# Talking-heads attention with two dense blocks: mixing weights spread by matmuls, first heads turned in column halves, two loads moved among stores

## The chip, the core and the metric

The kernel runs on one core of a Trainium2 chip. The metric is the device time of one execution in microseconds. Durations of single instructions and transfers come from one profiled execution.

## The reference

The attention works on 2 batches, 12 heads, 448 positions and 64 elements for each head, and mixes the heads twice: the scores before the softmax, and the softmax after it.

```python
scores = scale * np.matmul(q, k.transpose(0, 1, 3, 2))
scores = np.einsum('bhij,hg->bgij', scores, w_pre)
attn = softmax(scores)                                  # over j
attn = np.einsum('bhij,hg->bgij', attn, w_post)
x = np.matmul(attn, v)                                  # then (batch, position) x (head, element): 896 x 768
...
xn = x / sqrt(mean(x * x) + 1e-06) * rms_g
y = (silu(xn @ w_gate) * (xn @ w_val)) @ w_out          # 768 -> 1536 -> 768
out = elu(y @ w_in) @ w_out2                            # 768 -> 2048 -> 768
```

All inputs and the output are float32. `w_pre` and `w_post` are 12 x 12.

## The kernel before

The order of the work on every engine is written out by hand: an engine executes its instructions in program order, and a wait at one holds all that is behind it on that engine. All large transfers are issued by SyncE, in order, into one queue; the small ones of the start are issued by ScalarE.

**Opening.** `load_small` loads `w_pre` and `w_post` (12 x 12 each, into `wpp`) and two copies of them broadcast to 128 partitions (`wide`, `wpb`). `load_first` loads the six pairs of heads of q and k of the first batch, 224 KB each, alternately k and q. A position is split as 112 partitions times 4 chunks. The tiles of k lie as (chunk, head, element), so that each piece of a transfer is 64 floats, 256 bytes. The tiles of q lie as (head, chunk, element), so that a piece is 1024 bytes, and `q_beside` copies each of them on VectorE into the order of k. `busy(n)` puts n transposes of the identity, whose result nobody uses, on TensorE: 20 before the first pair, 8, 6, 4 and 4 between the turnings of the first two pairs.

Then a loop of eight trips runs over the pairs. Trip i turns k and q of pair i (`turned`, line 444: four transposes each, 112 positions by 128 columns that are two heads), and for pair i - 2 makes the premixed scores of the first two groups directly (`direct`, line 484, with q multiplied by the weights `wpq`, `mixed_q`) and the raw scores of the first 112 rows (`scores`, line 497). `follow` issues what ScalarE and VectorE have to do with the results. The matrices `m1` and `m2`, block diagonal copies of the weights for groups of 10 rows, come out of `select`, `repeat`, `copies` and `blocks`, in trip 1. `select` takes the largest value in each column of `w_post` from `wpb`.

**Way of the scores.** Raw scores of two heads and 112 rows are copied to a tile (`scores_out`; seven tiles in turn, four named `st_w` and three `st`) and stored in DRAM, `s_d`, 392 KB each; six of them make a block of 112 rows. `load_group` loads two groups (2 x 10 rows, all heads, 420 KB) back as `sg`, with four such tiles. Groups 0 and 1 don't take this way. Groups 2 to 5 are loaded after the opening (`AT_ONCE = 2` loads).

**Steps.** After the opening come the softmax of groups 0 and 1 (`soft`), six pairs of scores of the second row block (the loop over `EARLY`, one store each), and then the steps, counted by t from -4. Step t contains, among others, in this order, the load of groups t + 7 and t + 8 where t + 7 is even (AHEAD = 7), the premixing matmuls of group t + 1 (lines 582 or 585 to 587), the split of group t + 3 on ScalarE (`g_split`, line 574, even groups only), the exponential of group t (line 602) and the postmixing of group t - 3 (line 661). So groups 6 and 7 are loaded in step -1, as the first of the steps' loads, and split in step 3; groups 14 and 15 are loaded in step 7 and split in step 11. A window of 70 rows is closed by the product with v (`av`, line 697, f32, the two heads of a pair into the two halves of the output partitions). In between, pairs of heads of the second batch are loaded (`load_qk`, line 392, 256-byte pieces), turned and scored, and v is loaded (line 380). The two dense blocks follow.

Of the kernel before, what the change touches and what calls it, by code (L numbers as in the profile page):

```python
# [9 lines left out]
F32 = mybir.dt.float32  # L10
# [12 lines left out]
def block_kernel(  # L23
# [15 lines left out]
    nc = tc.nc  # L39
# [58 lines left out]
    def slot(p, *dims):  # L98
        a, n = taken[0], 1
        for d in dims:  # L100
            n *= d
        taken[0] += n
        t = setup[:p, a:a + n]
        return t.rearrange("p (a b) -> p a b", a=dims[0]) if len(dims) > 1 else t
# [1 line left out]
    m1 = slot(GP, GI, H)  # L106
    m2 = slot(GP, GI, H)
    wpp = slot(H, 2, H)
    wpb = slot(P, H * H)
    wpq = slot(P, H // 2, H)  # L110
    g_sb = const.tile([P, KD], F32, name="g_sb")
    g_dn = const.tile([P, KD], F32, name="g_dn")
# [2 lines left out]
    m2l = const.tile([GP, H, GI], F16, name="m2l")  # L115
    vsc = const.tile([P, KD], F32, name="vsc")

    def load_small(wide):
        nc.scalar.dma_start(out=wpp[:, 0], in_=w_pre)
        nc.scalar.dma_start(out=wpp[:, 1], in_=w_post)  # L120
        nc.scalar.dma_start(
            out=wide, in_=w_pre.rearrange("h g -> (h g)").unsqueeze(0).to_broadcast([P, H * H])
        )
        nc.scalar.dma_start(
            out=wpb, in_=w_post.rearrange("h g -> (h g)").unsqueeze(0).to_broadcast([P, H * H])
        )

    def mixing(m1f, m1h, m1l):

        selr, cmax, rcm, m2p = slot(H, GI, H), slot(P, H), slot(P, H), slot(GP, H, GI)  # L130
        a1 = m1.rearrange("p i g -> p (i g)")
# [238 lines left out]
    def attention(actx):  # L370
# [26 lines left out]
        def load_first():  # L397

            n_pair = 2 * NCH * D
            room = [ap.tile([CP, NCH * H * WMAX], F32, tag="at", name="qk0", bufs=2) for _ in range(2)]  # L400
            for p in range(NP):
                for j, (src, tag) in enumerate(((k, "kt"), (q, "qt"))):
                    a = (p % 3 * 2 + j) * n_pair
                    t = room[p // 3][:, a:a + n_pair]
                    if tag == "kt":
                        t = t.rearrange("p (c h d) -> p c h d", h=2, c=NCH)
                        nc.sync.dma_start(out=t, in_=pair_of(src, 0, p))
                    else:
                        t = t.rearrange("p (h c d) -> p h c d", h=2, c=NCH)
                        nc.sync.dma_start(  # L410
                            out=t, in_=src[0, 2 * p:2 * p + 2].rearrange("h (p c) d -> p h c d", c=NCH)
                        )
                    qk_sb[0, p, tag] = t

        def q_beside(p):

            t = ap.tile([CP, NCH, 2, D], F32, tag="qt", name="qt", bufs=2)
            nc.vector.tensor_copy(out=t, in_=qk_sb[0, p, "qt"].rearrange("p h c d -> p c h d"))
            qk_sb[0, p, "qt"] = t

        idle_ps = []

# [16 lines left out]
        def turned(b, p, tag):  # L439

            t = qk_sb.pop((b, p, tag))
            ps = ps_a()
            for c in range(NCH):
                nc.tensor.transpose(
                    out=ps[:, c * CP:(c + 1) * CP], in_=t[:, c].rearrange("p h d -> p (h d)"),
                    identity=ident[:CP, :CP],
                )
            hi, lo = parts_of(b, p, tag)
            on_act.append(lambda: nc.scalar.activation(out=hi, in_=ps[:, :S], func=ACTF.Copy))
            if b == 0 and tag == "qt":  # L450
                on_dve.append(lambda: mixed_q(p, ps))
            on_dve.append(
                lambda: nc.vector.tensor_tensor(out=lo, in0=ps[:, :S], in1=hi.bitcast(F32), op=ALU.subtract)
            )
# [328 lines left out]
        m1f = ap.tile([GP, GP], F32, tag="m1f", name="m1f", bufs=1)  # L783
        m1h = ap.tile([GP, GP], F32R, tag="m1h", name="m1h", bufs=1)
        m1l = ap.tile([GP, GP], F32R, tag="m1l", name="m1l", bufs=1)
        select, repeat, copies, blocks, _, pre, post = mixing(m1f, m1h, m1l)
        wide = ap.tile([P, KD, WMAX], F32, tag="sq", name="wide", bufs=1)[:, :3].rearrange("p k i -> p (k i)")[:, :H * H]
        load_small(wide)
        load_first()
        busy(20)  # L790
        q_beside(0)
        for s in range(2):
            nc.vector.tensor_copy(
                out=wpq[s * D:(s + 1) * D],
                in_=wide.rearrange("p (k s g) -> p s k g", s=2, g=H)[s * D:(s + 1) * D, s],
            )
        for i in range(NP + 2):
            if i < NP:
                turned(*pairs[i], "kt")
                if i < 2:  # L800
                    busy(8 - 4 * i)
                turned(*pairs[i], "qt")
                if i < 2:
                    busy(6 - 2 * i)
            if i == 1:
                select()
                repeat()
            if i > 1:
                direct(0, i - 2)
                scores(0, i - 2, 0, True)  # L810
            if i + 1 < NP:
                q_beside(i + 1)
            follow()
            if i == 1:
                copies()
                blocks()
        idle_ps.clear()
# [15 lines left out]
        for j in range(EARLY):  # L833
            if j in (0, 3):
                g_postmix(0, j // 3)
                g_out(0, j // 3)
            hq.pop(0)()
            follow()
        fast = len(hq)
        hq += [f for i in range(NP, 2 * NP) for f in turn(i)]  # L840
        turns = len(hq)
# [346 lines left out]
```

## Time and profile before

| | |
|---|---|
| median of 3 runs | 765.9 us (764.99 to 766.69) |
| profiled execution | 766.09 us |
| its span, first to last instruction | 764.3 us |
| TensorE busy | 746.3 us, 98% |
| VectorE busy | 549.2 us, 72% |
| ScalarE busy | 438.9 us, 57% |
| GpSimd busy | 100.3 us, 13% |
| mean granted TensorE clock | 0.994 of 2.4 GHz |
| moved by DMA | 103.68 MB, mean 136 GB/s |

The span is 1.8 us shorter than the profiled execution. A matmul's busy time overlaps with that of the next one, so a high share of TensorE is not the share of its peak. The chain of waits is followed back from the last instruction; idle time of an engine that is not on it costs nothing. In the rows below PE is TensorE's matmul, PEld its weight load, DVE VectorE, ACT ScalarE, POOL GpSimd, and SP SyncE; a q behind the name is the sequencer. L and a number is a line of the kernel.

### The profile page before, as it was taken

The page shows a single profiled execution, that of the slowest core. Times are in us where ns is not written, and L with a number is a line of the kernel's source. Part 1 is how long each engine was busy: PE and PEld are TensorE (multiplying, and loading weights), DVE is VectorE, ACT ScalarE, POOL GpSimd, SP SyncE. Part 2 cuts the span into 40 slices and gives each one's busy share as a digit, 9 for nine tenths or more (in the row PEclk, how much of TensorE's full clock was granted, in tenths as well). Part 3 has the DMA queues.
Part 4 walks back from the last instruction along what each step waited for, and adds up shares of the span by engine and source line. Part 5 has one row for each costly group of instructions (what it writes and reads, how often), then busy time and mean ns, then how long its engine had stood idle before and what let it go on. Part 6 is the DMA issues. An engine that isn't in the chain of part 4 may idle for free.

```text
span 764.3 us, 14562 instructions
## 1 busy us (share of the span) xinstructions
PE 746.3 (98%) x5740; PEld 590.6 (77%) x5740; DVE 549.2 (72%) x1094; ACT 438.9 (57%) x916; POOL 100.3 (13%) x122
## 2 busy tenths in 40 slices
PE   7979999999999999999999999999999999999997
PEld 6647887777777755555555599999999999999997
DVE  4757998988998757787886766554888778723731
ACT  4548788988988716666667423232766665312310
POOL 2122454443445300000000000000000000000000
PEclk9989999999999999999999999999999999999999
DMA  7699976878772013433332233241334334533602
GB/s 172 184 325 305 187 186 194 242 201 239 223 191 57 2 42 126 123 94 114 124 124 82 86 122 124 83 122 51 120 121 125 109 98 125 164 85 82 168 30 73
DMA packets 86616, 103.68 MB, mean 136 GB/s; under 512 B 20549, under 2 KB 77077, under 8 KB 86549
## 3 DMA queue, kind: packets, MB, share of 16 engines
q1 hardware_dynamic: 86213, 102.61, 47.0%
q8 instruction: 45, 0.74, 0.4%
q10 hardware_dynamic: 336, 0.15, 0.1%
q14 instruction: 22, 0.18, 0.1%
HBM read 80.72 MB, written 22.02 MB: 134 GB/s over the span
## 4 chain that ended last, share of the span: by engine, by line
PE 89%; DVE 4%; ACT 3%; DMA 3%; issue 1%; SPq 1%; ACTq 0%
PE psa_t L202 13%; PE psa_t L204 13%; PE psa_t L203 13%; PE pst_t L661 6%; PE psv_t L697 5%; PE psa_t L582 4%; PE psa_t L1144 4%; PE psa_t L1142 4%; PE psa_t L1143 4%; PE psa_t L497 4%; PE psf_t L202 3%; PE psf_t L204 3%; PE psf_t L203 3%; PE psa_t L585 2%; PE psf_t L1143 1%; PE psf_t L1142 1%
## 5 line engine op out<-in xcount | busy, mean ns | idle before, releaser
L661 PEld LDWEIGHTS <-eh 120*112 120x112 f16 x720 | 66.7, 131 | 25.4 <-issue 16.2
L257 ACT ACTIVATE whl<-w 128x768 fp32r<-128x768 f32 x44 | 37.2, 846 | 85.5 <-DVE w L251 74.9
L229 ACT ACTIVATE w<-raw 128x768 f32<-128x768 f32 x68 | 61.6, 908 | 25.4 <-DVE whl L309 18.9
L261 DVE TENSOR_TENSOR whl<-w,whl 128x768 fp32r<-128x768 f32 x44 | 42.2, 959 | 45.3 <-ACT whl L257 45.3
L204 PE MATMUL psa_t<-x2h,whl 128*128 128x448 f32 x192 | 70.5, 367 | 0.0
L202 PE MATMUL psa_t<-x2h,whl 128*128 128x448 f32 x192 | 70.1, 365 | 0.0
L203 PE MATMUL psa_t<-x2l,whl 128*128 128x448 f32 x192 | 69.8, 364 | 0.0
L575 POOL TENSOR_TENSOR sl<-sg,sh 120x448 fp32r<-120x448 f32 (+1 forms) x44 | 54.6, 1241 | 109.4 <-ACT sh L574 104.0
L602 ACT ACTIVATE e<-psa_t,nmax 120x448 f32<-120x448 f32 (+1 forms) x89 | 57.1, 642 | 19.3 <-DVE rs L617 16.0
L640 DVE SCALAR_TENSOR_TENSOR el<-e,rs,eh 120x448 f16<-120x448 f32 (+1 forms) x90 | 66.1, 734 | 0.1
L251 DVE SCALAR_TENSOR_TENSOR w<-w,raw 128x768 int32<-128x768 int32 x68 | 65.2, 959 | 1.1
L245 DVE SCALAR_TENSOR_TENSOR raw<-raw 128x768 int32<-128x768 int32 x68 | 65.7, 966 | 0.0
L661 PE MATMUL pst_t<-m2h,el 120*112 120x120 f16 x360 | 63.0, 218 | 1.6 <-DVE el L640 1.5
L661 PE MATMUL pst_t<-m2h,eh 120*112 120x120 f16 x360 | 63.2, 218 | 0.7 <-DVE eh L633 0.5
L661 PE MATMUL pst_t<-m2l,eh 120*112 120x120 f16 x360 | 63.1, 217 | 0.0
L301 ACT ACTIVATE w<-w,gs 128x128 f32<-128x128 f32 x144 | 44.6, 392 | 23.2 <-DVE gs L290 23.2
L594 DVE TENSOR_REDUCE nmax<-psa_t 120x1 f32<-120x448 f32 (+1 forms) x89 | 54.5, 612 | 0.2 <-PE psa_t L587 0.2
L673 ACT ACTIVATE at<-pst_t 112x480 f32<-112x480 f32 (+1 forms) x90 | 52.5, 583 | 3.5 <-PE pst_t L661 3.2
L697 PE MATMUL psv_t<-at,vs 112*64 112x70 f32 (+3 forms) x1344 | 54.2, 228 | 0.0
L1142 PE MATMUL psa_t<-whl,gh 128*128 128x384 f32 x160 | 54.0, 338 | 0.0
L1143 PE MATMUL psa_t<-whl,gh 128*128 128x384 f32 x160 | 54.0, 338 | 0.0
L1144 PE MATMUL psa_t<-whl,gl 128*128 128x384 f32 x160 | 54.0, 338 | 0.0
(158 smaller groups left out, 1900.4 us busy)
## 6 DMA issues: line engine op xcount, KB each, us to landing
raw<-in_moe_w_out_dram SPq DMA_DIRECT2D x28, 768.0 KB, 4.4
sg<-s_d SPq DMA_DIRECT2D x43, 420.0 KB, 6.1
s_d<-st SPq DMA_DIRECT2D x33, 392.0 KB, 3.6
raw<-in_moe_w_in_dram SPq DMA_DIRECT2D x16, 768.0 KB, 4.6
raw<-in_moe_w_gate_dram SPq DMA_DIRECT2D x12, 768.0 KB, 4.5
raw<-in_moe_w_val_dram SPq DMA_DIRECT2D x12, 768.0 KB, 4.4
s_d<-st_w SPq DMA_DIRECT2D x15, 392.0 KB, 4.9
vs<-in_v_dram SPq DMA_DIRECT2D x12, 224.0 KB, 6.4
```

The lines of the kernel that those rows point to most:

```text
L202: nc.tensor.matmul(out=ps, lhsT=wh(kk), rhs=xh_(kk), start=(first and kk == 0), stop=False)
L203: nc.tensor.matmul(out=ps, lhsT=wh(kk), rhs=xl_(kk), start=False, stop=False)
L204: nc.tensor.matmul(out=ps, lhsT=wl(kk), rhs=xh_(kk), start=False, stop=(last and kk == nk - 1))
L229: nc.scalar.activation(out=w, in_=raw.bitcast(F32)[:, :, 1], func=ACTF.Abs if small else ACTF.Copy, scale=REBASE)
L245: nc.vector.scalar_tensor_tensor(out=lo, in0=hi, scalar=SIGN, in1=lo, op0=ALU.bitwise_and, op1=ALU.bitwise_or)
L251: nc.vector.scalar_tensor_tensor(out=wi, in0=wi, scalar=3, in1=lo, op0=ALU.logical_shift_left, op1=ALU.bitwise_or)
L640: nc.vector.scalar_tensor_tensor(out=el[:r], in0=e32[:r], scalar=rs[:r], in1=eh[:r], op0=ALU.mult, op1=ALU.subtract)
L661: nc.tensor.matmul(out=o, lhsT=lhs[:r, c * CP:(c + 1) * CP], rhs=rhs[:r, :, :ni], start=(n == 0), stop=(n == 2),)
L697: nc.tensor.matmul(out=psx[s * D:(s + 1) * D, kk, :n], lhsT=vs[b, kk][:, s, c, :], rhs=at[:, c, hh, :n], start=(c == 0), stop=(c == NCH - 1),)
L1142: nc.tensor.matmul(out=o, lhsT=gh[:, kk, tk], rhs=wh[:, j], start=first, stop=False)
L1143: nc.tensor.matmul(out=o, lhsT=gh[:, kk, tk], rhs=wl[:, j], start=False, stop=False)
L1144: nc.tensor.matmul(out=o, lhsT=gl[:, kk, tk], rhs=wh[:, j], start=False, stop=end)
```

## The change

- `load_small` keeps the two 12 x 12 loads. The broadcasts are no longer transfers: `spread_small` builds selectors from the identity and two products of them with the weights on VectorE, multiplies on TensorE (K = 12, 72 and 144 columns), copies `wpq` out and leaves `wpb` in PSUM, where `select` reads it. `select` now comes before the loop, `repeat`, `copies` and `blocks` in trip 0. `spread_small` stands behind the 20 fillers and ahead of the first turning on TensorE.
- The tiles of k of the first batch lie as those of q, in 1024-byte pieces; `q_beside` goes.
- `turned` of the first batch makes, for each chunk and each head, a matmul of 112 x 64 stationary data with the identity, f32, into partitions 0 to 63 or 64 to 127, in place of one transpose for both heads. The second batch keeps its loads and transposes.
- In the loop over `EARLY`, the loads of groups 6 and 7 and of groups 8 and 9 are issued after the third and the sixth store of the second row block; `AT_ONCE` becomes 4, and the steps' loads begin with groups 10 and 11.

```diff
--- before.py
+++ after.py
@@ -106,7 +106,6 @@
     m1 = slot(GP, GI, H)
     m2 = slot(GP, GI, H)
     wpp = slot(H, 2, H)
-    wpb = slot(P, H * H)
     wpq = slot(P, H // 2, H)
     g_sb = const.tile([P, KD], F32, name="g_sb")
     g_dn = const.tile([P, KD], F32, name="g_dn")
@@ -115,17 +114,48 @@
     m2l = const.tile([GP, H, GI], F16, name="m2l")
     vsc = const.tile([P, KD], F32, name="vsc")
 
-    def load_small(wide):
+    def load_small():
         nc.scalar.dma_start(out=wpp[:, 0], in_=w_pre)
         nc.scalar.dma_start(out=wpp[:, 1], in_=w_post)
-        nc.scalar.dma_start(
-            out=wide, in_=w_pre.rearrange("h g -> (h g)").unsqueeze(0).to_broadcast([P, H * H])
+
+    def spread_small(wide):
+
+        at = [0]
+
+        def part(*dims):
+            n = 1
+            for d in dims:
+                n *= d
+            t = wide[:H, at[0]:at[0] + n]
+            at[0] += n
+            return t.rearrange("p (a b) -> p a b", a=dims[0]) if len(dims) > 1 else t
+
+        odd, of, sel = part(2), part(H // 2), part(2, D)
+        eye = ident[:H, :H]
+        nc.vector.tensor_reduce(out=odd, in_=eye.rearrange("h (p s) -> h s p", s=2), axis=AXX, op=ALU.add)
+        nc.vector.tensor_reduce(out=of, in_=eye.rearrange("h (p s) -> h p s", s=2), axis=AXX, op=ALU.add)
+        nc.vector.tensor_copy(out=sel, in_=odd.unsqueeze(2).to_broadcast([H, 2, D]))
+        own, eyed = part(H // 2, H), part(H, H)
+        nc.vector.tensor_tensor(
+            out=own, in0=of.unsqueeze(2).to_broadcast([H, H // 2, H]),
+            in1=wpp[:, 0].unsqueeze(1).to_broadcast([H, H // 2, H]), op=ALU.mult,
         )
-        nc.scalar.dma_start(
-            out=wpb, in_=w_post.rearrange("h g -> (h g)").unsqueeze(0).to_broadcast([P, H * H])
+        nc.vector.tensor_tensor(
+            out=eyed, in0=eye.unsqueeze(2).to_broadcast([H, H, H]),
+            in1=wpp[:, 1].unsqueeze(1).to_broadcast([H, H, H]), op=ALU.mult,
         )
-
-    def mixing(m1f, m1h, m1l):
+        ps, n = ps_a(), H * H // 2
+        nc.tensor.matmul(
+            out=ps[:, :n], lhsT=sel.rearrange("p s d -> p (s d)"), rhs=own.rearrange("p a b -> p (a b)"),
+            start=True, stop=True,
+        )
+        nc.tensor.matmul(
+            out=ps[:, n:3 * n], lhsT=ones[:H], rhs=eyed.rearrange("p a b -> p (a b)"), start=True, stop=True
+        )
+        nc.vector.tensor_copy(out=wpq.rearrange("p a b -> p (a b)"), in_=ps[:, :n])
+        return ps[:, n:3 * n]
+
+    def mixing(m1f, m1h, m1l, wpb):
 
         selr, cmax, rcm, m2p = slot(H, GI, H), slot(P, H), slot(P, H), slot(GP, H, GI)
         a1 = m1.rearrange("p i g -> p (i g)")
@@ -402,21 +432,9 @@
                 for j, (src, tag) in enumerate(((k, "kt"), (q, "qt"))):
                     a = (p % 3 * 2 + j) * n_pair
                     t = room[p // 3][:, a:a + n_pair]
-                    if tag == "kt":
-                        t = t.rearrange("p (c h d) -> p c h d", h=2, c=NCH)
-                        nc.sync.dma_start(out=t, in_=pair_of(src, 0, p))
-                    else:
-                        t = t.rearrange("p (h c d) -> p h c d", h=2, c=NCH)
-                        nc.sync.dma_start(
-                            out=t, in_=src[0, 2 * p:2 * p + 2].rearrange("h (p c) d -> p h c d", c=NCH)
-                        )
+                    t = t.rearrange("p (h c d) -> p h c d", h=2, c=NCH)
+                    nc.sync.dma_start(out=t, in_=src[0, 2 * p:2 * p + 2].rearrange("h (p c) d -> p h c d", c=NCH))
                     qk_sb[0, p, tag] = t
-
-        def q_beside(p):
-
-            t = ap.tile([CP, NCH, 2, D], F32, tag="qt", name="qt", bufs=2)
-            nc.vector.tensor_copy(out=t, in_=qk_sb[0, p, "qt"].rearrange("p h c d -> p c h d"))
-            qk_sb[0, p, "qt"] = t
 
         idle_ps = []
 
@@ -441,10 +459,14 @@
             t = qk_sb.pop((b, p, tag))
             ps = ps_a()
             for c in range(NCH):
-                nc.tensor.transpose(
-                    out=ps[:, c * CP:(c + 1) * CP], in_=t[:, c].rearrange("p h d -> p (h d)"),
-                    identity=ident[:CP, :CP],
-                )
+                o = ps[:, c * CP:(c + 1) * CP]
+                if b:
+                    nc.tensor.transpose(out=o, in_=t[:, c].rearrange("p h d -> p (h d)"), identity=ident[:CP, :CP])
+                    continue
+                for s in range(2):
+                    nc.tensor.matmul(
+                        out=o[s * D:(s + 1) * D], lhsT=t[:, s, c], rhs=ident[:CP, :CP], start=True, stop=True
+                    )
             hi, lo = parts_of(b, p, tag)
             on_act.append(lambda: nc.scalar.activation(out=hi, in_=ps[:, :S], func=ACTF.Copy))
             if b == 0 and tag == "qt":
@@ -783,17 +805,13 @@
         m1f = ap.tile([GP, GP], F32, tag="m1f", name="m1f", bufs=1)
         m1h = ap.tile([GP, GP], F32R, tag="m1h", name="m1h", bufs=1)
         m1l = ap.tile([GP, GP], F32R, tag="m1l", name="m1l", bufs=1)
-        select, repeat, copies, blocks, _, pre, post = mixing(m1f, m1h, m1l)
-        wide = ap.tile([P, KD, WMAX], F32, tag="sq", name="wide", bufs=1)[:, :3].rearrange("p k i -> p (k i)")[:, :H * H]
-        load_small(wide)
+        load_small()
         load_first()
+        wide = ap.tile([P, KD, WMAX], F32, tag="sq", name="wide", bufs=1).rearrange("p k i -> p (k i)")
         busy(20)
-        q_beside(0)
-        for s in range(2):
-            nc.vector.tensor_copy(
-                out=wpq[s * D:(s + 1) * D],
-                in_=wide.rearrange("p (k s g) -> p s k g", s=2, g=H)[s * D:(s + 1) * D, s],
-            )
+        wpb = spread_small(wide)
+        select, repeat, copies, blocks, _, pre, post = mixing(m1f, m1h, m1l, wpb)
+        select()
         for i in range(NP + 2):
             if i < NP:
                 turned(*pairs[i], "kt")
@@ -802,16 +820,13 @@
                 turned(*pairs[i], "qt")
                 if i < 2:
                     busy(6 - 2 * i)
-            if i == 1:
-                select()
+            if i == 0:
                 repeat()
             if i > 1:
                 direct(0, i - 2)
                 scores(0, i - 2, 0, True)
-            if i + 1 < NP:
-                q_beside(i + 1)
             follow()
-            if i == 1:
+            if i == 0:
                 copies()
                 blocks()
         idle_ps.clear()
@@ -836,6 +851,9 @@
                 g_out(0, j // 3)
             hq.pop(0)()
             follow()
+            if j in (2, EARLY - 1):
+                load_group(0, ND + AT_ONCE * LG)
+                AT_ONCE += 1
         fast = len(hq)
         hq += [f for i in range(NP, 2 * NP) for f in turn(i)]
         turns = len(hq)
```

## Rows read from the trace of the kernel before

**Rows 1.** The chain of waits from 30 to 50 us: start, length, what.

```profile
35.28 4.53 DMA s_d<-st
...
41.97 6.36 DMA sg<-s_d
```

**Rows 2.** Order of time, ScalarE's split: start, length; idle time before it.

```profile
48.41 0.58 ACT L574 ACTIVATE sh<-sg 120x448 fp32r<-120x448 f32 x1 [4.50 <-DMA sg<-s_d]
...
67.11 0.59 ACT L574 ACTIVATE sh<-sg 120x448 fp32r<-120x448 f32 x1
```

**Rows 3.** Order of time, TensorE, premixing from 49 to 62 us.

```profile
49.65 0.73 PE L585 MATMUL psa_t<-sh,m1h 120*120 120x448 f32 x1 [3.67 <-ACT e L602]
...
57.17 0.46 PE L585 MATMUL psa_t<-sh,m1h 120*120 120x448 f32 x1
...
61.74 0.47 PE L585 MATMUL psa_t<-sh,m1h 120*120 120x448 f32 x1
```

**Rows 4.** Windows of 10 us: busy time by engine, granted clock, DMA share, GB/s.

```profile
36.00:46.00 10.00, 9.20 (x53) 4.82 (x49) 6.26 (x13) 5.36 (x11) 2.26 (x2) 1.00 0.96 299
46.00:56.00 10.00, 6.35 (x31) 4.32 (x32) 5.74 (x17) 5.92 (x15) 2.27 (x2) 0.66 1.02 350
56.00:66.00 10.00, 10.00 (x92) 7.18 (x92) 6.55 (x19) 8.28 (x21) 2.27 (x2) 1.00 1.12 269
```

**Rows 5.** Order of time, opening: TensorE, and the small load's issue.

```profile
1.45 0.31 ACTq L120 DMA_DIRECT2D setup<-in_w_post_dram  x1
...
5.29 0.55 PE L444 MATMUL psa_t<-ident,qk 112*128 112x112 f32 x4
5.68 1.04 PE L428 MATMUL psv_i<-ident 128*128 128x128 f32 x8
...
9.88 0.60 PE L444 MATMUL psa_t<-ident,qk 112*128 112x112 f32 x4 [1.28 <-DMA qk<-in_k_dram]
10.32 0.60 PE L428 MATMUL psv_i<-ident 128*128 128x128 f32 x4
...
12.56 0.38 PE L145 MATMUL psa_t<-setup 12*120 12x24 f32 x2 [0.45 <-DVE setup L136]
12.87 0.60 PE L444 MATMUL psa_t<-ident,qk 112*128 112x112 f32 x4
...
15.70 0.60 PE L444 MATMUL psa_t<-ident,qk 112*128 112x112 f32 x4
...
16.46 0.84 PE L484 MATMUL psv_d<-par,mq 128*120 128x448 f32 x3
...
22.68 0.87 PE L484 MATMUL psv_d<-par,mq 128*120 128x448 f32 x3
```

**Rows 6.** DMA issues at 0.8, 1.8, 2.3, 59.21: KB, us to landing.

```profile
qk<-in_k_dram SPq DMA_DIRECT2D x1, 224.0 KB, 3.6
...
wide<-in_w_pre_dram ACTq DMA_DIRECT2D x1, 72.0 KB, 4.0
...
setup<-in_w_post_dram ACTq DMA_DIRECT2D x1, 72.0 KB, 6.6
...
sg<-s_d SPq DMA_DIRECT2D x1, 420.0 KB, 6.6
```

**Rows 7.** The copies of q: ns min/median/max, first and last start.

```profile
L418 DVE COPY qt<-qk x6: 363/428/676, 6.9 to 19.6; 112x512 f32<-112x512 f32 x6
```

**Rows 8.** Order of time, TensorE, products with v and one f32 premixing.

```profile
67.64 1.20 PE L697 MATMUL psv_t<-at,vs 112*64 112x70 f32 x32
...
73.61 0.71 PE L697 MATMUL psv_t<-at,vs 112*64 112x70 f32 x16
74.24 1.01 PE L582 MATMUL psa_t<-sg,m1f 120*120 120x448 f32 x2
```

**Rows 9.** Order of time, SyncE's DMA issues.

```profile
54.49 2.92 SPq L392 DMA_DIRECT2D qt<-in_q_dram  x1
...
59.21 0.95 SPq L546 DMA_DIRECT2D sg<-s_d  x1
```

## The prediction

> **What bounds the kernel now.** I read the chain of waits first, then the engines' order of time around each piece of it that is not TensorE, then the DMA views of the same stretch. After about 50 us the chain is almost without a break TensorE, VectorE and ScalarE work. Before that it holds two long DMA pieces, back to back but for some ScalarE work: the store of a raw score tile at 35.28 and the load of groups 6 and 7 at 41.97, 6.36 us to landing [rows 1]. ScalarE's first split of that load stands idle for 4.50 us in front of 48.41 [rows 2]; TensorE then stands idle for 3.67 us in front of 49.65, and from 49.65 to 57.17 it needs 7.52 us for two groups, where the next two take 4.57 [rows 3]. The windows say why: the granted clock is 0.66 over 46 to 56 us, so part of it at 1.2 GHz, and 1.00 in the windows beside it [rows 4]. So this place costs 3.67 + 2.95 = 6.6 us. But the same windows show DMA shares of 0.96, 1.02 and 1.12 from 36 to 66 us [rows 4]: the transfers, too, have no room there. The opening loop (the trips that turn a pair of heads) is the other stage touched. From 15.70 on a trip takes 2.33 us ((22.68 - 15.70) / 3) and TensorE goes from one piece to the next without a wait; before 12.87 it waits for data [rows 5].
>
> **The change, part by part.** *Loads of k and the removed copies.* Now the first k tile lands 3.6 us after its issue, before the 20 filler turns end at 5.29 [rows 5, 6]. With four times longer pieces it is at worst as early, and the later pairs, at which TensorE now waits (9.88, 1.28 us idle), come sooner; I take all waits for q and k in the opening as gone. The VectorE copies of q (428 ns each [rows 7]) go too, but in the trips they run beside TensorE, so that is worth nothing by itself.
>
> *Spread of the weights.* Two broadcasts of 72 KB leave ScalarE's queue; their landing was 4.0 and 6.6 us [rows 6]. Five small VectorE operations and two f32 products come in front of the first turning. One f32 product shows as two matmul instructions, and the nearest pair takes 0.31 us to the next work (12.56 to 12.87 [rows 5]); with up to 144 columns I take 0.5 us for both products. They need w_post, whose 0.6 KB landing the trace does not show; it is issued ahead of both broadcasts. I take it as landed before 5.29. The bound above is the later broadcast's 6.6 us, counted from the issue at 1.45 [rows 5], so 8.05, and one VectorE step of at most 0.43 us: 3.2 us late. Below, nothing.
>
> *Heads turned in halves.* This is the cost. A turning is four transposes now; 8 of them, a pair, take 0.76 us (15.70 to 16.46 [rows 5]). After, it is 8 ordinary f32 products, 16 instructions, each with 64 stationary and 112 moving columns. The nearest row is the product with v in the same form (112 x 64, halves of the output partitions in turn): 32 instructions with 70 columns in 1.20 us and 16 in 0.71, so (1.20 - 0.71) / 16 = 31 ns each, or 0.44 ns for a column [rows 8]. The f32 product without halves takes 1.01 us for two instructions of 448 columns [rows 8], at least 1 ns for a column, so the halves overlap. Scaled by 112 / 70 the price is 49 ns. Leaving this form costs (74.24 - 73.61) - 16 x 0.031 = 0.14 us [rows 8]. A turning is then 0.78 us, a pair 1.57 + 0.14 = 1.71 us in place of 0.76: 0.95 us more for each trip. No other engine has to follow: the trips lose VectorE work.
>
> Where the third trip starts: 5.29, plus 0.5 for the spread, 4 turnings at 0.92, 22 fillers at 0.11 (8 take 1.04 us and 4 take 0.60 [rows 5]), so 2.4, plus 0.31 for the moved selector product: 12.2, against 12.87. Four trips at 2.33 + 0.95 = 3.28 take 13.1 us, against 22.68 - 12.87 = 9.8. So the opening ends 13.1 - 9.8 - 0.6 = 2.7 us later; call it d. Bounds: 2.0 if leaving the form is free, 3.5 if entering it costs as much again. The VectorE work behind it (the rest of the weights, the first two softmaxes) starts with the copy of the last scores, in order, so all up to the store at 35.28 moves by d.
>
> The Trainium skill (TensorEngine Tiling (Array Packing), Restrictions and Gotchas) says that column tiling excludes transpose mode for f32, and TensorE: Matmul & The Clock Gate (Terms) puts that mode at four times the speed for f32. The rows above give a ratio near two for the pair of halves, because two run at once; by a ratio of four the sum would come to that of the third rival below.
>
> *Loads among the stores.* The load of groups 6 and 7 now stands behind seven stores of the second row block and after the change behind three. Four stores of 392 KB at 299 GB/s [rows 4] are 5.4 us, so it lands at 48.33 - 5.4 = 42.9 + d; ScalarE wants it at 43.91 + d [rows 2]. This stall goes, and with it the slow clock. Stores 4 to 6 move back by one load, 1.4 us; their tiles are wanted again only later.
>
> *What is late next.* Transfers go through one queue and keep their order afterwards. Between 54.49 and 57.41 the queue itself is held up while the 256-byte pieces of the second batch's q are issued, and groups 14 and 15 are issued behind them at 59.21 [rows 9], landing 6.6 us later, at 65.8 [rows 6]. ScalarE takes them at 67.11 [rows 2]: 1.3 us of slack now. The bytes ahead of that load do not change, and the DMA engines are full from 36 on, so it lands at 65.8 + d = 68.5. ScalarE would be there at 67.11 - 6.6 + d = 63.2 and waits 5.3 us. The stall is moved, not removed. At 48.41 TensorE idled 0.83 us less than ScalarE; so the net is 65.8 + 2.7 - 67.11 - 0.83 = +0.6 us, if the clock holds. Behind it TensorE carries the chain to the end, so this stays.
>
> **The sum** is made against the profiled execution: 766.09 us, its span of 764.3 and 1.8 around it, 0.2 above the median of 765.9. 766.1 + 0.6 = 766.7.
>
> **Rivals.** *The clock falls again* behind the moved stall. For: TensorE's idle time there is about 5.3 - 0.83 = 4.5 us, and 3.67 was followed by the lower level. Against: waits for the loads in between may break it into shorter ones, and 1.28 us at 9.88 left the clock alone. Price 2.95 again: 769.6, slower. It decides if the single idle stretch is as long as now.
> *DMA keeps up.* For: 46 to 56 moved 350 GB/s, the windows beside it 299 and 269; the 9.2 MB of 36 to 66 would take 26.2 us at 350, 3.8 less. Then 766.7 - 3.8 = 762.9, and without any new stall 766.1 - 6.6 + 2.7 = 762.2: faster. Against: the fast window holds mainly loads, and the slow one the 256-byte pieces, which remain.
> *The halves do not overlap*, 98 ns each: the first four turnings cost 3.1 us more, and the four trips 6.3 more: 766.7 + 9.4 = 776.
> *The weights land late*: d + 3.2, 769.9.
> *The early loads don't come early* (the queue waits for the stores in front of them): the stall stays, d comes on top: 768.8.
>
> **How the numbers follow.** Moved stall with the clock held, 0.33: mostly within 0.2%, which is 1.5 us and about what a measurement of this kernel can tell; 0.04 of it faster, 0.05 slower. Clock falls, 0.20, slower. DMA keeps up, 0.34: 0.29 faster, the rest within. Late weights, 0.06: 0.04 slower. No overlap, 0.04, slower. Loads not early, 0.03, slower. Together 0.33 faster, 0.31 same, 0.36 slower. The likeliest is 766.7, its own range 766.0 to 767.5 by the bounds of d. The range goes from 762.5, in the middle of the rival of DMA, to 770.0, over the fallen clock and the late weights.
>
> **What would show it.** A trip of 3.3 us and 16 instructions for each turning, about 50 ns apart; TensorE without idle time from 5.3 us on; the store now at 35.28 at about 38; no idle time of ScalarE at the split of groups 6 and 7; in its place idle time at groups 8 to 16, longest at 14; DMA share still about 1.0 from 39 to 69. The prediction is wrong if trips stay near 2.4 us, or if groups 14 and 15 land before 65.

## The result, and the profile after

The changed kernel takes 770.31 us (median of 4 executions, 769.80 to 770.96); the kernel before, timed beside it, 766.3 us (4 executions, 764.99 to 766.71). The ratio is 1.0054, with an interval of 1.0038 to 1.0069: slower by 4.0 us. The forecast was 766.7, no change, and the measured median lies 0.3 us above the upper end of its range. The profiled execution of after took 770.5 us, its span 768.8.

First the opening: TensorE of after in order of time (start, length, line, tiles, instructions; in brackets idle time before).

```profile
1.42 4.53 PE L446 MATMUL psv_i<-ident 128*128 128x128 f32 x20 [1.42 <-POOL ident masks.py:199]
5.88 0.44 PE L148 MATMUL psa_t<-wide 12*128 12x72 f32 x2
6.16 0.45 PE L152 MATMUL psa_t<-wide,ones 12*128 12x144 f32 x2
6.54 0.99 PE L467 MATMUL psa_t<-ident,qk 112*64 112x112 f32 x16
7.46 1.09 PE L446 MATMUL psv_i<-ident 128*128 128x128 f32 x8
8.48 0.99 PE L467 MATMUL psa_t<-ident,qk 112*64 112x112 f32 x16
...
13.52 1.75 PE L467 MATMUL psa_t<-ident,qk 112*64 112x112 f32 x32
15.21 0.88 PE L506 MATMUL psv_d<-par,mq 128*120 128x448 f32 x3
...
26.64 0.87 PE L506 MATMUL psv_d<-par,mq 128*120 128x448 f32 x3
```

From 1.42 us to the end of these rows TensorE does not stand idle, where in before it waited for data and for copies [rows 5]. A turning is 16 instructions and 0.92 us to the next work (6.54 to 7.46). Four trips run from 13.52 to 26.64, 3.28 us each, as forecast; but the third trip starts at 13.52, not at the forecast 12.2. The copy of the last scores comes at 29.96 in place of 26.00, and the first store of the second row block is issued at 39.23 in place of 35.28: **d is 3.96 us in this execution, not 2.7**.

The small weights were not late: they are used before the 20 fillers end at 5.88. VectorE of after in order of time has the two products that need w_pre and w_post:

```profile
3.14 0.22 DVE L139 TENSOR_TENSOR wide<-wide,setup 12x72 f32<-12x72 f32 x1 [1.34 <-DMA setup<-in_w_pre_dram]
4.51 0.30 DVE L143 TENSOR_TENSOR wide<-ident,setup 12x144 f32<-12x144 f32 x1 [1.15 <-DMA setup<-in_w_post_dram]
```

ScalarE's split of the groups (order of time; after's L596 is before's L574), to be held against [rows 2]:

```profile
47.72 0.57 ACT L596 ACTIVATE sh<-sg 120x448 fp32r<-120x448 f32 x1
52.62 0.58 ACT L596 ACTIVATE sh<-sg 120x448 fp32r<-120x448 f32 x1 [2.18 <-DMA sg<-s_d]
57.37 0.58 ACT L596 ACTIVATE sh<-sg 120x448 fp32r<-120x448 f32 x1 [0.27 <-DMA sg<-s_d]
64.39 0.58 ACT L596 ACTIVATE sh<-sg 120x448 fp32r<-120x448 f32 x1 [2.56 <-DMA sg<-s_d]
72.45 0.58 ACT L596 ACTIVATE sh<-sg 120x448 fp32r<-120x448 f32 x1 [4.00 <-DMA sg<-s_d]
76.81 0.58 ACT L596 ACTIVATE sh<-sg 120x448 fp32r<-120x448 f32 x1
```

These are groups 6, 8, 10, 12, 14 and 16. The wait of 4.50 us at group 6 is gone, and group 6 is split 0.69 us earlier than before (47.72 against 48.41) though all in front of it is 3.9 us late: 4.6 us won. The waits at groups 8 to 14 are 9.0 us together and take it back: group 14 is 5.34 us later than before (72.45 against 67.11), group 16 is 4.24 later, and from group 20 to group 36 the distance is 4.26 to 4.32. The spans differ by 4.5 us.

The windows of after (columns as in [rows 4]; two of 10 us, then four of 2 us) show transfers and clock:

```profile
46.00:56.00 10.00, 9.55 (x67) 5.97 (x66) 7.17 (x23) 7.24 (x20) 2.27 (x2) 1.00 0.98 340
66.00:76.00 10.00, 8.85 (x91) 6.30 (x90) 5.18 (x19) 5.66 (x16) 1.30 (x2) 0.83 0.97 300
...
62.00:64.00 2.00, 1.60 (x19) 1.10 (x17) 0.23 (x1) 0.00 (x0) 0.00 (x0) 1.00 1.20 130
...
66.00:68.00 2.00, 1.80 (x17) 1.24 (x15) 2.00 (x8) 1.65 (x6) 0.18 (x1) 0.84 0.88 220
68.00:70.00 2.00, 2.00 (x18) 1.36 (x20) 0.92 (x2) 0.45 (x1) 0.00 (x0) 0.50 0.83 260
70.00:72.00 2.00, 2.00 (x29) 1.49 (x26) 0.00 (x0) 0.00 (x0) 0.00 (x0) 0.81 1.06 368
```

The slow stretch of before, 0.66 over 46 to 56 us, is gone; in its place the granted clock falls at 66 to 72 us, to 0.50, all at 1.2 GHz, over 68 to 70. TensorE had stood idle for 2.03 us in front of 65.63. The DMA share is near 1 over both 10 us windows, but below 0.9 from 66 to 70 us; and at 62 to 64 us, at a share of 1.20, only 130 GB/s are moved. That is where the queue issues the 256-byte pieces of q. SyncE's issues in order of time, to be held against [rows 9]:

```profile
39.23 0.32 SPq L548 DMA_DIRECT2D s_d<-st  x1
...
59.15 4.64 SPq L422 DMA_DIRECT2D qt<-in_q_dram  x1
...
65.21 0.69 SPq L568 DMA_DIRECT2D sg<-s_d  x1
```

The issue of q holds the queue for 4.64 us instead of 2.92, and the load of groups 14 and 15 is issued 6.0 us later than before (65.21 against 59.21). The later first store makes 3.95 us of that; the other 2.05 us come up in the queue behind it (26.0 us from the first store to this load, 23.9 in before). The load lands at 72.36, not at the forecast 68.5. The Trainium skill (DMA: Bandwidth & Descriptors, Specifications) asks for at least 512 bytes a piece for the full rate; the trace agrees, with 130 GB/s at 62 to 64 against 368 at 70 to 72. Of the packets of these two windows 1092 of 1186 and 34 of 405 are under 512 bytes.

The chain of waits of after goes from that load on to the next transfer that TensorE waits for, the k of the second pair of the second batch (start, length, what):

```profile
65.21 7.15 DMA sg<-s_d
...
76.47 0.30 SPq L548
76.83 7.75 DMA kt<-in_k_dram
```

Between the two stand ScalarE's exponentials and copies of scores: k is issued behind a store (76.47) that waits for them. On TensorE (order of time; first after, then before) this looks as follows:

```profile
73.69 1.29 PE L519 MATMUL psa_t<-par 64*112 64x448 f32 x6 [0.95 <-ACT e L624]
...
75.54 0.46 PE L607 MATMUL psa_t<-sh,m1h 120*120 120x448 f32 x1
...
84.63 0.60 PE L464 MATMUL psa_t<-ident,kt 112*128 112x112 f32 x4 [0.31 <-DMA kt<-in_k_dram]
```

```profile
71.78 0.46 PE L585 MATMUL psa_t<-sh,m1h 120*120 120x448 f32 x1
...
80.39 0.56 PE L444 MATMUL psa_t<-ident,kt 112*128 112x112 f32 x4
```

The premixing of group 14 is 3.76 us later than before (75.54 against 71.78), and the turning of that k 4.24 us (84.63 against 80.39). So the load of groups 14 and 15 brings most of the delay, and the wait for k adds 0.5 us.

### The profile page after: what moved, and what is told of

The parts are those of the page before. It is cut to its first block, busy times and chain, and to the rows that moved or that the text cites. A ratio compares the mean times of both kernels' runs of the same rounds, so it can differ in the third digit from the quotient of the medians.

```text
span 768.8 us, 14854 instructions
## 1 busy us (share of the span) xinstructions
PE 753.0 (98%) x5888; PEld 596.5 (78%) x5888; DVE 547.9 (71%) x1092; ACT 439.3 (57%) x916; POOL 99.6 (13%) x122
## 4 chain that ended last, share of the span: by engine, by line
PE 87%; DMA 4%; ACT 3%; DVE 3%; issue 1%; SPq 1%; POOL 0%; ACTq 0%; POOLq 0%; DVEq 0%
PE psa_t L232 13%; PE psa_t L234 13%; PE psa_t L233 13%; PE pst_t L683 5%; PE psv_t L719 5%; PE psa_t L1161 4%; PE psa_t L1162 4%; PE psa_t L1160 4%; PE psf_t L234 3%; PE psf_t L233 3%; PE psf_t L232 3%; PE psa_t L604 3%; PE psa_t L519 3%; DMA sg<-s_d 2%; PE psf_t L1160 1%
## 5 line engine op out<-in xcount | busy, mean ns | idle before, releaser
L291 DVE TENSOR_TENSOR whl<-w,whl 128x768 fp32r<-128x768 f32 x44 | 42.2, 959 | 45.3 <-ACT whl L287 45.3
```

## The experiments

All differences are to the kernel before, timed on the same chip (765.9 us for e1 to e4, 766.1 for e5 to e8, 766.39 for e9 to e12).

**e1: the moved loads alone**, on the kernel before.

```diff
             hq.pop(0)()
             follow()
+            if j in (2, EARLY - 1):
+                load_group(0, ND + AT_ONCE * LG)
+                AT_ONCE += 1
```

> The kernel before, with only the loads of groups 6 to 9 moved among the stores. Theory (the stall is moved to the load of groups 14 and 15, since the queue's bytes ahead of it do not change): no idle time of ScalarE at the split of groups 6 and 7, idle time of 3 to 5 us at groups 12 to 16 instead, and a time within 2 us of before, 764 to 768. Rival (the early loads are worth their stall and the slower clock, and only the late opening spoilt it): about 6 us faster, 760.

766.41 us, ratio 1.0006 (0.9989 to 1.0022): no change. ScalarE does not wait at group 6 (44.04); in order of time it waits further on:

```profile
48.77 0.58 ACT L574 ACTIVATE sh<-sg 120x448 fp32r<-120x448 f32 x1 [1.90 <-DMA sg<-s_d]
...
67.61 0.58 ACT L574 ACTIVATE sh<-sg 120x448 fp32r<-120x448 f32 x1 [3.57 <-DMA sg<-s_d]
```

Five waits make 8.0 us, and group 14 is split 0.5 us later than before. The load of groups 14 and 15 is issued 26.0 us behind the first store of the second row block, as in after, and lands at 67.53, where before had 65.8. The rows are from the chain of waits, then TensorE in order of time, then a window:

```profile
61.55 5.98 DMA sg<-s_d
...
70.71 0.56 PE L585 MATMUL psa_t<-sh,m1h 120*120 120x448 f32 x1
...
74.73 1.01 PE L582 MATMUL psa_t<-sg,m1f 120*120 120x448 f32 x2
...
66.00:76.00 10.00, 7.97 (x80) 6.04 (x79) 6.26 (x21) 7.28 (x18) 2.26 (x2) 0.83 1.04 360
```

TensorE premixes group 14 1.07 us earlier than in before (70.71 against 71.78) and group 15 0.49 us later (74.73 against 74.24 [rows 8]). In between the granted clock is lower, 0.50 over 72 to 74 us, after 2.03 us of idle time in front of 68.85. So what is won at group 6 goes to the later waits and, for the last 1.5 us, to the clock.

**e2: the new opening alone**, the changed kernel without those three lines.

```diff
-            if j in (2, EARLY - 1):
-                load_group(0, ND + AT_ONCE * LG)
-                AT_ONCE += 1
```

> The changed kernel without the moved loads: only the opening is changed. Theory (the opening ends 4 us later and all behind it is moved by that, the stall at groups 6 and 7 with it): 4 us slower than before, 770, the stall of 4.5 us at groups 6 and 7 at about 52 us as before. Rival (part of the delay is hidden in the stall, because the transfers go on meanwhile): under 2 us slower.

770.09 us, ratio 1.0064 (1.0041 to 1.0088). The stall at group 6 is there again, 4.55 us in front of 52.40, 4.0 us later than before. The whole loss is the opening's; the moved loads are worth nothing with it and nothing without it.

**e3: the second batch's first pair loaded later**, to take its 256-byte pieces from ahead of groups 14 and 15.

```diff
             if t == 5:
                 nc.sync.dma_start(out=g_sb, ...)
+            if t == 9:
                 load_qk(*pairs[NP])
```

> The changed kernel with the first pair of the second batch loaded in step 9, behind the load of groups 16 and 17, not in step 5. Theory (the 4 us wait at groups 14 and 15 is the order in the queue, the 256-byte pieces in front of it): that wait goes, and the time falls by 3 to 5 us, to 765.5 to 767.5. Rival (it is the bytes that bind, whatever their order): the wait moves to groups 16 to 20 or to the turning of that pair, and the time stays within 1 us of 770.3.

770.93 us, ratio 1.0061 (1.0038 to 1.0085); the four executions lie between 768.41 and 771.96. The wait at group 14 is gone (split at 69.60), and the time is not better. The granted clock was 0.58 and 0.56 over 68 to 72 us, after 1.28 us of idle time, and the chain of waits then holds the next pair's k. VectorE's copy of the last scores, then TensorE, in order of time:

```profile
32.02 0.62 DVE L543 COPY st<-psa_t 112x448 f32<-112x448 f32 x1 [2.56 <-PE psa_t L519]
...
84.67 0.60 PE L464 MATMUL psa_t<-ident,kt 112*128 112x112 f32 x4 [0.64 <-DMA kt<-in_k_dram]
```

The profile can't be read as the time is, for the same opening ended 2.06 us later in it than in that of after (32.02 against 29.96; the pace of its first turnings is lower, see the last section), and still the turning of that k comes only 0.04 us later. From the first store of the second row block to this turning it takes 43.4 us here, 45.4 in after, 45.1 in before, 44.9 in e2, 45.3 in e1 and 45.8 in e4. So in this execution the edit took 2.0 us out of the stretch. From 278.5 us, where the profile is 0.06 us behind that of after, to 500 us it loses 1.4 us more; its granted clock is 0.91 over 280 to 300, where after has 1.00. The 3 to 5 us that were expected show in none of the four executions (the lowest is 1.9 us under after's median). Whether the edit is worth some 2 us stays open, and so does whether another transfer would hold after as long if groups 14 and 15 came earlier.

**e4: whole transposes in after**, from tiles that VectorE (q) and GpSimd (k) bring into the other order first.

```diff
+        def beside(p):
+            for tag, eng in (("kt", nc.gpsimd), ("qt", nc.vector)):
+                t = ap.tile([CP, NCH, 2, D], F32, tag=tag, name=tag, bufs=2)
+                eng.tensor_copy(out=t, in_=qk_sb[0, p, tag].rearrange("p h c d -> p c h d"))
+                qk_sb[0, p, tag] = t
...
-                for s in range(2):
-                    nc.tensor.matmul(
-                        out=o[s * D:(s + 1) * D], lhsT=t[:, s, c], rhs=ident[:CP, :CP], start=True, stop=True
-                    )
+                nc.tensor.transpose(out=o, in_=t[:, c].rearrange("p h d -> p (h d)"), identity=ident[:CP, :CP])
...
+        beside(0)
...
+            if i + 1 < NP:
+                beside(i + 1)
```

> The changed kernel, but the first batch is turned by four transposes for a tile again: VectorE copies each q tile and GpSimd each k tile into the order that a transpose needs; spread, pieces of 1024 bytes and moved loads stay. Theory (the matmuls in halves cost 0.95 us for each of four trips and 0.5 for each of four turnings ahead of them): the copy of the last first-block scores falls from 29.96 to 24 to 26 us, and the time is 764 to 767. Rival (the opening is late because of what was put in front of the first turning): it ends after 28 us and the time stays above 768.5.

767.36 us, ratio 1.0021 (0.9998 to 1.0044): 1.5 us above before, where after is 4.0 above. The copy of the last scores comes at 26.05, as in before and not earlier, since the third trip waits for GpSimd (TensorE in order of time):

```profile
12.98 0.60 PE L470 MATMUL psa_t<-ident,kt 112*128 112x112 f32 x4 [2.29 <-POOL kt L443]
```

The four selections that `blocks` issues from 10.42 to 12.04 us stand ahead of that copy.

**e5: the loads and fewer bytes in the full stretch**, on the kernel before: the v tiles of the first batch are loaded right behind `load_first`, and the second batch's first pair ahead of groups 2 to 5. **e10: the same without the moved loads** (the three lines from `if j in` on). **e6: the same two moves in after**, the pair right behind `load_first` too.

```diff
         load_first()
+        for kk in range(KD):
+            load_v(0, kk)
...
         hq = [f for c in range(1, NCH) for f in rows(0, c)]
+        load_qk(*pairs[NP])
...
+            if j in (2, EARLY - 1):
+                load_group(0, ND + AT_ONCE * LG)
+                AT_ONCE += 1
...
-            if 0 <= t - 3 < KD:
-                load_v(0, t - 3)
             if t == 5:
                 nc.sync.dma_start(out=g_sb, ...)
-                load_qk(*pairs[NP])
```

> The kernel before with the moved loads of groups 6 to 9, and besides with v of the first batch loaded right behind the first q and k, and the first pair of the second batch loaded ahead of groups 2 to 5. Theory (transfers are the bound from 36 to 66 us and idle in the opening, so what is taken out of that stretch removes the waits of ScalarE at groups 8 to 16): those waits, 8.0 us in the run with the moved loads alone, fall under 2 us, and the time falls to 759.5 to 763. Rival (no bound of transfers, the waits have another cause, such as one load's own length): they stay and the time is 765 to 767.

> The kernel before with v and the first pair of the second batch loaded early, and without the moved loads. Theory (two things bound that stretch in turn, the place of the load of groups 6 and 7 behind seven stores, and the bytes ahead of groups 14 and 15): the stall of 4.5 us at groups 6 and 7 stays, the slow clock with it, and the time stays at 765 to 767; each of the two edits alone gives nothing, together 6 us. Rival (the bytes alone are the bound): the stall falls under 2 us, 761 to 763.

> The changed kernel with v of the first batch and the first pair of the second batch loaded right behind the first q and k. Theory (as above): the waits of ScalarE, 9.0 us after the change, go with the slow clock behind them, 764 to 767; what stays is the late opening of 4 us less the removed stall. Rival (only the order matters, a later load waits in its place): 769 to 771.

e5: 760.03 us, ratio 0.9919 (0.9904 to 0.9934). e10: 765.53, 0.9984 (0.9968 to 0.9999), with the stall at group 6 still there (4.66 us). e6: 764.10, 0.9980 (0.9969 to 0.9991). The windows of e5 (columns as before):

```profile
20.00:30.00 10.00, 10.00 (x60) 7.09 (x59) 6.63 (x18) 5.80 (x14) 1.88 (x3) 1.00 0.95 298
...
56.00:66.00 10.00, 10.00 (x125) 7.51 (x124) 8.34 (x29) 9.08 (x24) 2.28 (x2) 1.00 0.98 336
66.00:76.00 10.00, 10.00 (x134) 8.13 (x131) 8.87 (x24) 7.62 (x20) 2.76 (x3) 1.00 1.03 244
```

The bytes now move at 20 to 30 us, where before had a share of 0.64; ScalarE waits for loads 1.9 us in all, none from group 12 on, and the clock is 1.00. The moved loads alone win nothing (e1), the early bytes alone 0.9 us (e10), both together 6.1: two limits stood behind one another. In e6 ScalarE waits for loads 2.3 us in all, none from group 12 on either; it keeps after's opening, and lies 4.1 us above e5. So the opening's price is there where these waits are gone.

**e7: after without the 22 filler turns between the first turnings.**

```diff
                 turned(*pairs[i], "kt")
-                if i < 2:
-                    busy(8 - 4 * i)
                 turned(*pairs[i], "qt")
-                if i < 2:
-                    busy(6 - 2 * i)
```

> The changed kernel without the 22 filler transposes between the first turnings. Theory (TensorE is busy without a break from 1.4 us on, so the fillers that once stood in waits now cost their full length, 3.0 us): the third trip starts at 10.5 us in place of 13.5, and the time falls by 2 to 3.5 us, 767 to 768.3. Rival (the data or the clock needs that time: the third pair is not there, or the clock stays low longer): less than 1 us.

768.90 us, ratio 1.0028 (1.0011 to 1.0045): 2.8 us above before, where after is 4.0 above. That is a gain of 1.2, less than the 2 to 3.5 us expected, and the fillers take 3.0. In its profile the opening ends only 1.2 us earlier than in that of after, for the first two turnings run at half the pace (TensorE in order of time):

```profile
7.08 3.25 PE L467 MATMUL psa_t<-ident,qk 112*64 112x112 f32 x32
```

That the missing fillers cause this is not shown: in e3, with the fillers, the pace is half up to 10.52 too.

**e8: e4 with the moves of e5**, and `blocks` in the last trip that turns. **e9: e8 without the 22 fillers** (the edit of e7).

```diff
             if i == 0:
                 copies()
+            if i == NP - 1:
                 blocks()
```

> The run with copies and whole transposes, with the four block selections on GpSimd moved behind the copies of k (they held up the third pair by 2.3 us), and with v and the first pair of the second batch loaded early. Theory: the third trip starts before 11.5 us in place of 12.98, the waits of ScalarE at groups 8 to 16 go, 758 to 761.5, faster than both kernels. Rival (the waits are only moved again, or GpSimd's copies hold the trips): 764 to 767.

> The run with copies and early loads of v, without the 22 filler transposes between the first turnings. Theory (the fillers are on the path there too): the third trip starts 1 to 2.4 us earlier and the time falls to 757.5 to 759. Rival (without them the clock stays low for longer, as in the changed kernel without fillers, and the data come no sooner): 759.5 to 761.

e8: 759.97 us, ratio 0.9918 (0.9894 to 0.9942), as e5 and 4.1 us under e6. Its third trip, which was expected before 11.5 us, starts at 13.60 in the profile, where the fillers ran at half pace (1.91 us for eight). e9: 761.30, ratio 0.9930 (0.9906 to 0.9955), in the range of its rival; the intervals of e8 and e9 overlap. Its third trip starts at 12.41, 1.2 us earlier than e8's, but runs at a lower pace up to 16.6, and the first store of the second row block is issued 0.7 us later (36.65 against 35.97). With whole transposes no gain from removing the fillers shows.

**e11: the spread alone**, on the kernel before: `spread_small`, `select` ahead of the loop, `repeat`, `copies` and `blocks` in trip 0; k, q, transposes and `q_beside` stay. **e12: e11 with the edits of e5.**

```diff
-        load_small(wide)
+        load_small()
         load_first()
...
         busy(20)
+        wpb = spread_small(wide)
+        select, repeat, copies, blocks, _, pre, post = mixing(m1f, m1h, m1l, wpb)
+        select()
         q_beside(0)
...
-            if i == 1:
-                select()
+            if i == 0:
                 repeat()
```

> The kernel before with the spread of the weights by matmuls alone (and the selectors moved ahead of the loop with it); loads, pieces and turnings as before. Theory (in that opening TensorE waits for data after the first turnings, so 0.7 us put in front of them is hidden): within 1 us of before. Rival (the spread, with its wait for the weights, is a main part of the late opening): 2 us slower or more.

> The kernel before with the spread, the moved loads, and v and the first pair of the second batch loaded early. Theory (the spread takes 144 KB of broadcasts out of the first transfers and the selectors out of the third trip, where VectorE held TensorE): 758.5 to 760.5, at least as fast as the same without the spread, 760.0. Rival (the spread costs its 0.7 us in front): 760.5 to 761.5.

e11: 764.13 us, ratio 0.9975 (0.9959 to 0.9990): the spread is a gain of 2.3 us, where within 1 us of before was expected. Its opening (TensorE in order of time):

```profile
6.94 0.61 PE L474 MATMUL psa_t<-ident,qk 112*128 112x112 f32 x4
7.38 1.04 PE L458 MATMUL psv_i<-ident 128*128 128x128 f32 x8
8.26 0.55 PE L474 MATMUL psa_t<-ident,qt 112*128 112x112 f32 x4
...
11.41 0.55 PE L474 MATMUL psa_t<-ident,qk 112*128 112x112 f32 x4
...
13.68 0.61 PE L474 MATMUL psa_t<-ident,qk 112*128 112x112 f32 x4
```

The third trip starts at 11.41, 1.46 us earlier than before, and takes 2.27 us where before needs 2.83 (12.87 to 15.70 [rows 5]): 2.0 us. Against e11, after's opening differs by k's pieces, the copies of q left out and the halves. Its third trip starts 2.1 us later (13.52) and its four trips take 4 x (3.28 - 2.33) = 3.8 us more, 5.9 together; by the times it is 4.2 (e2) + 2.3 (e11) = 6.5. So k's pieces, the halves and the fillers that no longer stand in waits eat the spread's gain and 4 us besides; these parts were not run one by one. e12: 757.64 us, ratio 0.9886 (0.9855 to 0.9917), the best kernel, 8.8 us under before. It has everything in the change but k's pieces, the halves and the dropped copies of q, and the bytes moved. No wait for transfers shows on TensorE from 46 to 66 us any more (windows of e12):

```profile
46.00:56.00 10.00, 9.99 (x86) 6.80 (x85) 7.38 (x23) 8.11 (x22) 2.27 (x2) 1.00 0.99 329
56.00:66.00 10.00, 10.00 (x125) 7.53 (x124) 8.58 (x28) 9.11 (x23) 2.28 (x2) 1.00 1.00 347
```

Over all profiles, the time from the issue of the first store of the second row block to the end of the span hardly depends on the opening: 729.0 us in before, 729.1 in e1, 729.2 in e2, 729.6 in after, 728.9 in e3, 729.9 in e4, 729.2 in e7, 728.1 in e10 and 729.6 in e11. With the moved loads and the early bytes together it is 722.6 in e5, 723.3 in e6, 722.8 in e8, 723.7 in e9 and 722.8 in e12. What the opening loses, the end loses too; the two moves together take some 6.5 us out of what is behind.

## Why the prediction was right and wrong

- **The price of a turning, right.** Forecast 16 instructions of 49 ns, 0.92 us with leaving the form, a trip of 3.28; measured 0.92 and 3.28. The halves overlap; that rival is refuted, and so is that of the late weights (4.51 us).
- **The start of the third trip, mis-sized.** Forecast 12.2, measured 13.52: 1.3 us short. The 20 leading fillers end at 5.88, not 5.29 (+0.6; 4.53 us for them where the trace of before had 4.03); the spread takes 0.66, not 0.5; the fillers between turnings take 1.02, 0.80, 0.59 and 0.58, 3.0 us and not 2.4, some 0.15 us for each entry into the half form from a filler. The forecast had that entry at nothing, and only in the upper bound of d at a price; with the other two it makes 3.96, above that bound of 3.5. (Eight times 0.14 us is 1.1, so by the forecast's own terms the bounds were 1.6 and 3.8; 3.96 is above that too.) The leading fillers are chance in part: the same 20 take 3.69 us to the next work in e6 and 4.46 in after. In the trips the entry costs nothing that shows (3.28 without it).
- **The stall at groups 6 and 7 goes, right; it moves, right.** e1 shows both without the opening. That the loads don't come early is refuted (group 6 at 47.72 without a wait), and so is that DMA keeps up (9.0 us of waits at the loads behind).
- **Where it moves to, right; when that load lands, mis-sized. This step failed.** "The bytes ahead of that load do not change, and the DMA engines are full from 36 on, so it lands at 65.8 + d = 68.5": it landed at 72.36. Of the 3.9 us, 1.3 are d. The other 2.6 came up behind the first store: the load was issued 2.05 us later after it than in before, with the issue of q holding the queue 1.7 us longer, and took 7.15 us in place of 6.6, while the DMA share was below 0.9 at 66 to 70 us. e1 shows the same with a d of only 0.28: issued 2.06 us later after the first store, and landed 1.7 us later than in before. With the measured landing the forecast's own sum gives 72.36 - 67.11 - 0.83 = 4.4 us, and the end is 4.0 us (medians) to 4.5 us (spans) late. Why the queue was held longer stays open; the transfers in front of that load are the same as in before, in another order.
- **The slack, right in kind.** The load landed 6.56 us later than before and TensorE's premixing of group 14 came 3.76 later, so 2.8 us vanished there; the forecast had 2.1. "Behind it TensorE carries the chain to the end" is not quite so: the wait for the second pair's k adds 0.5 us.
- **The sum.** The miss of 3.6 us (770.31 against 766.7) is 1.3 for d and 2.6 for the landing, less 0.7 for the larger slack, and 0.5 for k: 3.7.
- **The fallen clock.** That rival's time, 769.6, is near the measured one, and the clock did fall, after 2.03 us of idle time, not 4.5. Of the 6 us from 66 to 72 about 3.4 were at 1.2 GHz (0.32 + 1.00 + 0.38 of 2 us each). But in after it is not what the end waited for: behind the slow stretch TensorE still stood idle for 0.95 us in front of 73.69, until an exponential that stands behind the split of group 14 on ScalarE. So the nearness of 769.6 is luck. In e1, where that load landed earlier, the lower clock took the last 1.5 us. e6 has no such stretch, its clock is 1.00, and it lies 4.1 us above e5 all the same. How much of after's loss would have stayed had the clock held was not tried.
- **Without a new stall** the forecast had 766.1 - 6.6 + d. With after's d that is 763.5; e6 is 764.1, and e5, without d, 760.0 against 759.5. The price of the stall with its slow clock, 6.6, was about right.

## What to carry to other kernels

Where transfers run at a share near 1 over a stretch, a wait removed inside it can come back at the next loads, as here in e1 and after, unless bytes are moved to a stretch that has room (a share of 0.64 here). Work that delayed the stretch's start delayed the end by about as much, with the bytes moved (e6) and without (e2, after). Don't take the landing of a later load as fixed when loads ahead of it are reordered: here it was issued 2 us later with the same bytes in front. Once the waits in front of an engine are gone, fillers and slower forms that stood in them are on the path and have to be counted again. Price each part of a bundle alone: here one part won 2.3 us and, by subtraction, the rest of the opening lost about 6, and only the sum was visible.

## What the runs showed of the hardware that was not expected

TensorE's pace at the start differs between executions of the same instructions. In after the first turning takes 0.92 us and the eight fillers behind it 1.02; e3 has the same opening, and its profile (TensorE in order of time) shows

```profile
7.08 1.76 PE L467 MATMUL psa_t<-ident,qk 112*64 112x112 f32 x16
8.78 1.81 PE L446 MATMUL psv_i<-ident 128*128 128x128 f32 x8
10.52 0.99 PE L467 MATMUL psa_t<-ident,qk 112*64 112x112 f32 x16
```

that is 1.70 and 1.74 us, and the full pace only from 10.52 on: 2 us lost on the way to the third trip. The granted clock of that stretch is given as 1.00 in both (windows of e3):

```profile
6.00:11.00 5.00, 5.00 (x38) 4.27 (x40) 1.59 (x6) 0.54 (x1) 0.00 (x0) 1.00 1.12 264
```

So the record does not show what the durations show. The Trainium skill (TensorE: Matmul & The Clock Gate, Part 1) says that the number of slow matmuls at a kernel's start varies from run to run, which fits; that it is the clock here, no row proves. Before, waits for data stood behind the first turnings (1.28 us in front of 9.88 [rows 5]), and the first store of the second row block is issued at 35.28 to 35.87 in all four profiles with that opening (before, e1, e5, e10); with after's opening it is issued at 38.49 to 41.29 (after, e2, e3, e6). It also means that single profiles of these openings compare only within some 2 us, and the medians carry the verdicts.
